# Two-level products for two of four blocks in groups 4 to 6 of a fused attention and feed-forward kernel on Trainium2

## The chip, the cores and the metric

The kernel runs on one NeuronCore of a Trainium2 chip. Its engines work from queues of their own: TensorE multiplies matrices (PE; its weight loads are listed as PEld), VectorE (DVE) and ScalarE (ACT) work on tensors and read the matmul results in PSUM, GpSimd (POOL) works on SBUF alone, and SyncE (SP) issues most transfers. The metric is the device time of the launch in microseconds (us), smaller being better.

## The reference, cut to what matters

```python
kv = np.einsum('bhsd,bhse->bhde', k, v)          # b, h, s, d = 8, 8, 576, 64
out = np.einsum('bhsd,bhde->bhse', q, kv)
rms = np.sqrt(np.mean(out * out, axis=-1, keepdims=True) + 1e-06)
x = (out / rms * g_norm)                         # -> (4608 tokens, 512)
a = x @ w1                                       # 512 -> 1024
b = x @ w2
return (a * b @ w3) @ w_out                      # 1024 -> 1024 -> 512
```

Everything is float32.

## The kernel before, in words

w3 @ w_out is multiplied out first (the first 83 us). Then come nine groups of 512 tokens: groups 0 to 7 hold 512 tokens of one batch each, and group 8 holds the 64 leftovers of all eight batches. Their order is 0 to 6, 8, 7.

**Gates.** A group first computes a and b (*gates*, line 770). The 1024 features are four *blocks* p = 0 to 3, each of two times 128 features. A block is a two-by-two product in Strassen-Winograd form: seven products instead of eight, over halves of features, of the contraction and of tokens. Per block that is 28 matmuls of 128x128 by 128x256 (line 646). ScalarE evicts banks into *late* tiles (*keep*, line 657), and VectorE adds, forms a * b (*multiply*, lines 784 and 785) and writes the pieces c12, c22, c11 and c21 of ab. The weights' sums s1, s2, s4 lie in tiles ws0 to ws3, and the tokens' sums t1 to t4 in xc (made by *combine_x*).

**Two blocks at two levels.** Groups 8 and 7 (TWICE) do block 2 in that form, then blocks 0 and 1 together in *gates_of_two* (line 851): the seven outer products are each split again into seven matmuls of 128x128 by 128x128, for w1 and then w2, 98 in all (line 875). The inner sums of tokens are made on GpSimd (*sum_x*, line 827). The inner sums of weights are made during groups 3 and 4 (*prepare_w*), stored in DRAM, and loaded back in parts of 896 KB (*load_w*); *replace_a21* makes the fourth kind in place in group 6. VectorE adds and combines the results (lines 893 to 910). Block 3 follows, with VectorE in written order.

**Projection.** The group then multiplies by w3 @ w_out at two levels (*project_twice*, line 1040, matmuls on line 1075), with weights streamed by *load_b*; VectorE makes sums of ab just ahead (*sum_inner*, lines 1033 to 1037).

**Attention of the next batch.** While group T runs, batch T + 1 is prepared in eight pieces (*steps*, line 519), which *between* (line 1302) puts between products, two in each block: k v products, the q kv product of each half (*finish*), and for odd batches that of two batches' leftovers (*product_left*). *norm* squares on ScalarE, reduces on VectorE, takes a root on ScalarE, a reciprocal and a product on VectorE. q and x are turned by DMA: a copy that parts 16-bit halves, a DMA transpose issued by SP, a copy back (*turn_by_dma*, lines 296 to 310); from batch 2 on all these copies are GpSimd's.

**Order.** TensorE, GpSimd and SP run in written order throughout. VectorE does in the last block and the projection of a group, and from gates_of_two on in groups 8 and 7. Elsewhere VectorE's and ScalarE's order is set when the kernel is built, by readiness and then by written order; *issue_after* keeps an instruction behind a named one of its engine. Tiles of a pool with one buffer make the next writer wait for the last reader; the pool *ps_mm* has five PSUM banks, and *ps_at* three.

## Time and profile before

| what | value |
|---|---|
| time, median of 3 runs | 758.19 us (758.11 to 759.98) |
| profiled execution: its own time, its span | 758.72 us, 756.9 us |
| group 4, gates (390.8 to 445.2), VectorE / ScalarE / GpSimd busy | 54.4 us, 38.85 / 16.09 / 22.79 us |
| group 5, gates (467.08 to 520.64) | 53.56 us, 30.32 / 15.15 / 19.75 us |
| group 6, gates (542.5 to 595.37) | 52.87 us, 33.83 / 15.06 / 20.90 us |
| group 5, projection (520.64 to 542.5) | 21.86 us, 20.63 / 5.12 / 0 us |
| DMA | 143.2 MB, mean 189 GB/s |

The profile is of one execution. A row of a group of instructions gives line, engine, operation, output and input by the program's names, shape and count; then busy time, mean time of one, and idle time ahead with its cause. The chain of waits goes back from the last instruction, at each step to what released it. Rows of busy time by stage give for each engine the busy time and, in brackets, the instructions; then the granted clock, the share of time the transfers took, and their GB/s. In the timeline the columns are start, duration, engine, line, operation, operands and shape.

### The profile page before, as it was taken

The page shows a single profiled execution, that of the slowest core. Times are in us where ns is not written, and L with a number is a line of the kernel's source. Part 1 is how long each engine was busy: PE and PEld are TensorE (multiplying, and loading weights), DVE is VectorE, ACT ScalarE, POOL GpSimd, SP SyncE. Part 2 cuts the span into 40 slices and gives each one's busy share as a digit, 9 for nine tenths or more (in the row PEclk, how much of TensorE's full clock was granted, in tenths as well). Part 3 has the DMA queues.
Part 4 walks back from the last instruction along what each step waited for, and adds up shares of the span by engine and source line. Part 5 has one row for each costly group of instructions (what it writes and reads, how often), then busy time and mean ns, then how long its engine had stood idle before and what let it go on. Part 6 is the DMA issues. An engine that isn't in the chain of part 4 may idle for free.

```text
span 756.9 us, 14948 instructions
## 1 busy us (share of the span) xinstructions
PE 749.4 (99%) x5903; PEld 657.7 (87%) x5903; DVE 589.4 (78%) x1171; ACT 267.0 (35%) x492; POOL 164.1 (22%) x190
## 2 busy tenths in 40 slices
PE   8999999999999999999999999999999999999998
PEld 5455788888899889988998899889988999999997
DVE  7977999639888568758975897567776778996897
ACT  6777787312322232223222322232223223222321
POOL 0000000322511441144114410431143124006000
PEclk9999999999999999999999999999999999999999
DMA  9996954349997845675767567745743470465244
GB/s 319 344 334 177 273 163 102 85 104 271 336 299 248 225 114 177 223 205 141 218 218 210 155 192 223 208 103 173 224 125 53 150 225 28 146 211 186 87 152 139
DMA packets 146554, 143.20 MB, mean 189 GB/s; under 512 B 86580, under 2 KB 133812, under 8 KB 146484
## 3 DMA queue, kind: packets, MB, share of 16 engines
q1 hardware_dynamic: 144032, 127.82, 58.1%
q10 hardware_dynamic: 2452, 14.42, 5.7%
q8 instruction: 47, 0.77, 0.4%
q14 instruction: 23, 0.19, 0.1%
HBM read 105.78 MB, written 19.14 MB: 165 GB/s over the span
## 4 chain that ended last, share of the span: by engine, by line
PE 97%; DVE 1%; DMA 1%; ACT 1%; issue 0%; SPq 0%; ACTq 0%
PE mm L646 55%; PE mm L1075 23%; PE mm L625 7%; PE mm L875 5%; PE at L339 3%; PE at L415 2%; PE at L612 1%; PE at L875 1%; DMA raw<-in_moe_w_out_dram 1%; PE at L1126 0%; DVE ab L163 0%; PE at L358 0%; PE at L434 0%; DVE chunks L170 0%; SPq L198 0%
## 5 line engine op out<-in xcount | busy, mean ns | idle before, releaser
L646 PE MATMUL mm<-xT,w_sb 128*128 128x256 f32 x720 | 165.2, 380 | 0.0
L646 PEld LDWEIGHTS mm<-xT,w_sb 128*128 128x128 f32 x720 | 136.6, 191 | 18.3 <-issue 0.5
L646 PE MATMUL mm<-xc,ws 128*128 128x256 f32 x512 | 116.2, 380 | 0.0
L646 PEld LDWEIGHTS mm<-xc,ws 128*128 128x128 f32 x512 | 97.3, 190 | 13.7 <-ACT p L659 0.8
L296 POOL COPY xT<-xn 128x1024 uint16<-128x1024 uint16 x26 | 31.2, 1227 | 171.9 <-DVE xn L393 171.9
L784 DVE TENSOR_TENSOR c<-mm,u 128x512 f32<-128x512 f32 x32 | 22.0, 689 | 58.4 <-PE mm L646 58.4
L659 ACT COPY u<-mm 128x512 f32<-128x512 f32 x58 | 34.0, 585 | 93.4 <-PE mm L646 82.8
L659 ACT COPY p<-mm 128x512 f32<-128x512 f32 x66 | 38.7, 586 | 73.9 <-PE mm L646 68.5
L646 PE MATMUL mm<-xc,w_sb 128*128 128x256 f32 x256 | 61.4, 383 | 0.0
L625 PE MATMUL mm<-chunks,ab 128*128 128x512 f32 x128 | 60.1, 603 | 1.0 <-DVE chunks L173 1.0
L646 PE MATMUL mm<-xT,ws 128*128 128x256 f32 x240 | 57.4, 383 | 0.0
L785 DVE TENSOR_TENSOR ab<-c 128x256 f32<-128x256 f32 x96 | 53.8, 561 | 2.5
L646 PEld LDWEIGHTS mm<-xc,w_sb 128*128 128x128 f32 x256 | 48.0, 190 | 6.9 <-ACT u L659 0.3
L646 PEld LDWEIGHTS mm<-xT,ws 128*128 128x128 f32 x240 | 45.1, 190 | 6.2
L1075 PE MATMUL mm<-w3o_sb,ab 128*128 128x128 f32 x368 | 48.7, 276 | 0.0
L1075 PE MATMUL mm<-w3o_sb,raw 128*128 128x128 f32 x372 | 48.1, 276 | 0.0
L384 DVE TENSOR_REDUCE inv<-sq 128x8 f32<-128x512 f32 (+1 forms) x40 | 23.4, 627 | 30.0 <-ACT sq L383 30.0
L1075 PEld LDWEIGHTS mm<-w3o_sb,ab 128*128 128x128 f32 x368 | 45.4, 192 | 0.5
L780 ACT COPY c<-mm 128x256 f32<-128x256 f32 x32 | 11.9, 372 | 95.4 <-PE mm L646 95.4
L1075 PEld LDWEIGHTS mm<-w3o_sb,raw 128*128 128x128 f32 x372 | 44.8, 192 | 0.0
L1086 ACT COPY u<-mm 128x512 f32<-128x512 f32 x23 | 13.5, 586 | 85.3 <-DVE raw L1099 46.6
L310 POOL COPY xT<-xn 128x1024 uint16<-128x1024 uint16 x26 | 31.6, 1244 | 54.0 <-DMA xn<-xT 54.0
(300 smaller groups left out, 1378.7 us busy)
## 6 DMA issues: line engine op xcount, KB each, us to landing
w3o_sb<-w3o_l SPq DMA_DIRECT2D x18, 896.0 KB, 5.4
raw<-in_moe_w_dram SPq DMA_DIRECT2D x31, 512.0 KB, 7.1
raw<-w3o_l SPq DMA_DIRECT2D x15, 896.0 KB, 4.7
w3o_sb<-w3o_l ACTq DMA_DIRECT2D x14, 896.0 KB, 4.6
k_sb<-in_k_dram SPq DMA_DIRECT2D x32, 256.0 KB, 4.5
v_sb<-in_v_dram SPq DMA_DIRECT2D x32, 256.0 KB, 4.7
q_sb<-in_q_dram SPq DMA_DIRECT2D x32, 256.0 KB, 3.3
out_dram<-raw SPq DMA_DIRECT2D x14, 512.0 KB, 4.3
```

Of the source, the lines that this page charges most:

```text
L296: copy(to, src.rearrange("p a n w -> p w a n"))
L310: copy(words(dst), src)
L339: nc.tensor.matmul(kv_ps[e * D:(e + 1) * D, r - rs[0], :], lhsT=k_sb[:, e, cols] if j < J else kl[:, 2 * r + e, :], rhs=v_sb[:, e, cols] i ...
L384: nc.vector.tensor_reduce(out=inv[:, i], in_=sq.rearrange("p (h d) -> p h d", d=D), axis=AX.X, op=ALU.add)
L415: nc.tensor.matmul(o_ps[l][tokens, n * D:(n + 1) * D], lhsT=qT[r][rows, e, i, tokens], rhs=kv_b[rows, e, r, :], start=True, stop=True,)
L625: nc.tensor.matmul(sums_ps[half][m], lhsT=w3T[half, c][:, m, :], rhs=chunks[:, c, 1, :], start=(c == 0), stop=(c == KF - 1),)
L646: nc.tensor.matmul(ps[:, u, :], lhsT=lhsT(a_name, u, c), rhs=rhs(b_name, c),  start=(u == 0 and c == 0 and to is None), stop=(c == chunks ...
L659: copies.setdefault(name, []).append(nc.scalar.copy(t, ps))
L784: adds.setdefault(name, []).append(nc.vector.tensor_add(c, one, two))
L785: nc.vector.tensor_mul(dst, c[:, 0, :], c[:, 1, :])
L875: nc.tensor.matmul(ps[place // 4][:, place % 4, :], lhsT=x, rhs=y, start=new and place // 4 not in seen, stop=True, skip_group_check=True,)
L1075: nc.tensor.matmul(to[:, i, :], lhsT=x[:, c, :], rhs=y[:, c, :], start=new and place // 4 not in seen, stop=(c == 1), skip_group_check=True,)
```

## The change

- Groups 4, 5 and 6 too take blocks 0 and 1 in *gates_of_two* (IN_TWO; block 2 first, then the two, then block 3). The eight pieces of attention lie there: two in block 2, after products 2 and 5 of each w in the two-level part, two in block 3.
- For batches 5 to 7 the copies of the turnings are ScalarE's, each behind a named bank copy (*turns_by_scalar*, *run_slot*). Leftovers' products of odd batches (5 and 7) move to the first piece of block 3. The copies of their turning stay GpSimd's.
- *sum_x* is eight VectorE operations in place of 28 of GpSimd, behind the last output add of the group before, into ws0, ws1 and a square buffer. For that, all inner weight blocks of outer s1, s2 and s4 are stored and loaded too: 66 blocks of 128 columns in five parts, three loaded ahead and two inside the stage.
- *gates_of_two* takes five banks of ps_mm, with none of ps_at, and only the late tiles p1, p5 and u.
- Squares have two named buffers up to batch 4 and one from batch 5 on.
- *prepare_w* runs in its seven steps, one at a time (two in one place), from group 1 to 3, and *replace_a21* in group 3.

The diff, cut to its core:

```diff
@@ -62,6 +62,7 @@
+    FIRST_OF_TWO = 4
...
@@ -359,27 +360,27 @@
-        def q_by_dma(r):
+        def q_by_dma(r, copy=None):
...
-            return turn_by_dma([q_sb], to, q_sb, [to], q_copy)
+            return turn_by_dma([q_sb], to, q_sb, [to], copy or q_copy)
...
-        def q_left_by_dma():
+        def q_left_by_dma(copy=None):
...
-            return turn_by_dma([src], to, src, [to], q_copy)
+            return turn_by_dma([src], to, src, [to], copy or q_copy)
         def norm(o_ps, dsts):
...
-                sq = work.tile([P, G], FP32, name="sq")[:, 0:w]
+                sq = work.tile([P, G], FP32, name=f"sq{0 if b > FIRST_OF_TWO else i}", bufs=1)[:, 0:w]
...
@@ -450,19 +451,18 @@
-        def x_by_dma(h, copy=nc.gpsimd.tensor_copy):
+        def x_part_by_dma(h, r, copy):
...
-            half = [slice(r * G, (r + 1) * G) for r in range(2)]
-            return together(
-                turn_by_dma(
-                    [xn[:, :, r * P:(r + 1) * P]], flat[:, half[r]], turned[:, half[r]], [x[:, :, r]],
-                    copy,
-                )
-                for r in range(2)
+            half = slice(r * G, (r + 1) * G)
+            return turn_by_dma(
+                [xn[:, :, r * P:(r + 1) * P]], flat[:, half], turned[:, half], [x[:, :, r]], copy
...
+        def x_by_dma(h, copy=nc.gpsimd.tensor_copy):
+            return together(x_part_by_dma(h, r, copy) for r in range(2))
...
@@ -516,6 +516,54 @@
         return batches[b]
+    slots, stage = {}, [None]
+    def run_slot(key, behind):
+        for f, *args in slots.pop(key, []):
+            with tc.issue_after(behind.ins):
+                f(*args)
+    def turns_by_scalar(b):
+        a, turning = batch(b), {}
+        def at(key, *call):
+            slots.setdefault(key, []).append(call)
+        def begin(name, f, *args):
+            turning[name] = f(*args, nc.scalar.copy)
+            next(turning[name])
+            if name[0] == "q":
+                next(turning[name])
+            elif name[2]:
+                for r in range(2):
+                    next(turning["x", name[1], r])
+        def end(name):
+            all_of(turning[name])
+            if name[0] == "q" and name[1] != "left":
+                batch(name[1]).load_ahead("q", name[2])
+        for r in (2, 3):
+            at((0, 0), begin, ("q", b, r), a.q_by_dma, r)
+        if b % 2:
+            at(("p2", "c21"), begin, ("q", "left"), a.q_left_by_dma)
+            at((0, 3), end, ("q", "left"))
+        at((0, 6), end, ("q", b, 2))
+        at((1, 0), end, ("q", b, 3))
+        for h, begins, ends in (
+            (0, ((0, 3), (0, 3)), ((1, 3), (1, 3))),
+            (1, (("p3", "p1"), ("p3", "p5")), (("p3", "c21"), ("proj", "p1"))),
+        ):
+            for r in range(2):
+                at(begins[r], begin, ("x", h, r), a.x_part_by_dma, h, r)
+                at(ends[r], end, ("x", h, r))
+        if b + 1 < B:
+            n = batch(b + 1)
+            for r in range(2):
+                at(("p3", "u2"), begin, ("q", b + 1, r), n.q_by_dma, r)
+                at(("proj", ("u2", "u3")[r]), end, ("q", b + 1, r))
...
@@ -543,6 +591,7 @@
         odd = b % 2
+        by_scalar = b > FIRST_OF_TWO
...
@@ -577,6 +626,8 @@
+        elif by_scalar:
+            turns_by_scalar(b)
         else:
...
@@ -587,16 +638,20 @@
         if odd:
-            fs[second].append((a.product_left,))
+            fs[6 if by_scalar else second].append((a.product_left,))
...
-            turn(5, a.x_by_dma, 1)
+            if not by_scalar:
+                turn(5, a.x_by_dma, 1)
             if odd:
-                turn(5, a.x_left_by_dma, next_group=more)
+                turn(7 if by_scalar else 5, a.x_left_by_dma, next_group=more or by_scalar)
+                if by_scalar and not more:
+                    slots["proj", "p5"] = [to_end.pop()]
+        if more and not by_scalar:
+            turn(7 if b == 1 else 5, batch(b + 1).q_two_by_dma, 0, 1, next_group=True)
         if more:
-            turn(7 if b == 1 else 5, batch(b + 1).q_two_by_dma, 0, 1, next_group=True)
             fs[7 if odd else 0].append((load_q_left, b + 1))
...
@@ -657,6 +712,7 @@
         def keep(name, ps):
...
+            run_slot((stage[0], name), copies[name][-1])
...
@@ -777,7 +833,8 @@
             if two is None:
...
-                nc.scalar.copy(c, one[:, 0, :])
+                copied = nc.scalar.copy(c, one[:, 0, :])
+                run_slot((stage[0], name), copied)
...
@@ -793,6 +850,24 @@
+    PRODUCTS = [
+        ("a11", "b11"), ("a12", "b21"), ("s2", "t2"), ("s1", "t1"), ("s3", "t3"), ("s4", "b22"),
+        ("a22", "t4"),
+    ]
+    BLOCKS = {}
+    for w in range(2):
+        for n, (name, _) in enumerate(PRODUCTS):
+            keys = ("a11", "a12", "a22", "s3") if name in ("s1", "s2", "s4") else ()
+            for key in (*keys, "s1", "s2", "s4"):
+                BLOCKS[w, n, key] = len(BLOCKS)
+    IN_PART = PART // P
+    W_PARTS = -(-len(BLOCKS) // IN_PART)
+    def store_w(n, key, src):
+        dst = w_l2[:, 0:len(BLOCKS) * P].rearrange("p (w m) -> p w m", w=2)
+        at = BLOCKS[0, n, key] * P
+        nc.sync.dma_start(out=dst[:, :, at:at + P], in_=src)
...
@@ -802,71 +877,76 @@
-            for i, s in enumerate((s1, s2, s4)):
-                at = (3 * n + i) * 2 * P
-                nc.sync.dma_start(
-                    out=w_l2[:, at:at + 2 * P].rearrange("p (w m) -> p w m", w=2), in_=s
-                )
+            blocks = {"s1": s1, "s2": s2, "s4": s4, "a11": a11, "a12": a12, "a22": a22}
+            for key, t in blocks.items():
+                if (0, n, key) in BLOCKS:
+                    store_w(n, key, t)
...
     def replace_a21():
-        for name, _ in PRODUCTS:
+        for n, (name, _) in enumerate(PRODUCTS):
...
+            if (0, n, "s3") in BLOCKS:
+                store_w(n, "s3", a21)
...
     def load_w():
...
+        if n == W_PARTS:
+            return
...
-        nc.sync.dma_start(out=t, in_=w_l2[:, n * PART:(n + 1) * PART])
+        t = t[:, 0:min(PART, len(BLOCKS) * P - n * PART)]
+        nc.sync.dma_start(out=t, in_=w_l2[:, n * PART:n * PART + t.shape[1]])
...
     def sum_x(T):
...
-            for name in ("k_sb", "v_sb", "q_sb"):
-                for _ in range(2):
-                    x_sums.append(inp.tile([P, 2, J * D], FP32, name=name))
-            x_sums.append(work.tile([P, 2, 2, P], FP32, name="qT"))
-            x_sums[:] = [
-                t.rearrange("p a b -> p (a b)") if len(t.shape) == 3 else
-                t.rearrange("p a b c -> p (a b c)") for t in x_sums
-            ]
-            x_sums[:] = [[t[:, i * P:(i + 1) * P] for i in range(4)] for t in x_sums]
-        nc.gpsimd.tensor_copy(tick, late["p1"][:, 0, 0:1])
-        for t, (_, name) in zip(x_sums, PRODUCTS):
-            b11, b12, b21, b22 = (
-                xb[T][name][:, c, i * P:(i + 1) * P] for c in range(2) for i in range(2)
-            )
-            t1, t2, t3, t4 = t
-            nc.gpsimd.tensor_sub(t1, b12, b11)
-            nc.gpsimd.tensor_sub(t2, b22, t1)
-            nc.gpsimd.tensor_sub(t3, b22, b12)
-            nc.gpsimd.tensor_sub(t4, b21, t2)
-    places = []
-    def gates_of_two(T):
-        if not places:
-            other = work.tile([P, 2, 2, NP // 2, N], FP32, name="xT")
-            other = other.rearrange("p i j r n -> p (i j r n)")
-            places.extend([other[:, 0:PART // 2], other[:, 1024:1024 + PART // 2]])
-            places[:] = [t.rearrange("p (n t) -> p n t", t=P) for t in places]
+            of_xc, of_xT = (free["w", p] for p in range(2))
+            of_xc, of_xT = (t.rearrange("p s w c m -> p (s w c m)") for t in (of_xc, of_xT))
+            x_sums.append([
+                *(of_xT[:, i * 4 * P:(i + 1) * 4 * P].rearrange("p (n t) -> p n t", t=P) for i in range(3)),
+                work.tile([P, G], FP32, name="sq1", bufs=1).rearrange("p (n t) -> p n t", t=P),
+            ])
+            x_sums.append([
+                of_xc[:, i * 3 * P:(i + 1) * 3 * P].rearrange("p (n t) -> p n t", t=P) for i in range(4)
+            ])
+        whole = xT[T].rearrange("p i j c n -> p (i j) c n"), xc
+        for (t1, t2, t4, t3), x in zip(x_sums, whole):
+            b11, b12, b21, b22 = (x[:, :, c, i * P:(i + 1) * P] for c in range(2) for i in range(2))
+            nc.vector.tensor_sub(t1, b12, b11)
+            nc.vector.tensor_sub(t2, b22, t1)
+            nc.vector.tensor_sub(t3, b22, b12)
+            nc.vector.tensor_sub(t4, b21, t2)
+    X_OUTER = {"b11": (0, 0), "t3": (0, 1), "b21": (0, 2), "b22": (0, 3), "t1": (1, 0), "t2": (1, 1), "t4": (1, 2)}
+    def gates_of_two(T, between=lambda: None):
+        mm = [bank(ps_mm, "mm").rearrange("p (i n) -> p i n", n=P) for _ in range(5)]
+        plan = [((0, 1), (2, 3), (4, 2)), ((3, 4), (2, 0), (1, 2))]
+        names = [("p1", "p5", "u2", "p1"), ("u2", "p5", "p1", "u2")]
...
-            a11, a12, s3, a22 = (t[:, w] for t in w_blocks(a_name))
-            s1, s2, s4 = (
-                loaded_w[q // 7][:, q % 7 * 2 * P + w * P:q % 7 * 2 * P + (w + 1) * P]
-                for q in range(3 * n, 3 * n + 3)
-            )
+            def block(key):
+                at = BLOCKS[w, n, key]
+                return loaded_w[at // IN_PART][:, at % IN_PART * P:(at % IN_PART + 1) * P]
+            if (w, n, "s3") in BLOCKS:
+                a11, a12, s3, a22 = (block(key) for key in ("a11", "a12", "s3", "a22"))
+            else:
+                a11, a12, s3, a22 = (t[:, w] for t in w_blocks(a_name))
+            s1, s2, s4 = (block(key) for key in ("s1", "s2", "s4"))
...
-            t1, t2, t3, t4 = x_sums[n]
+            of, i = X_OUTER[b_name]
+            t1, t2, t4, t3 = (t[:, i] for t in x_sums[of])
...
@@ -877,16 +957,23 @@
-            if w == 1 and n in (2, 4, 6):
-                load_b()
+            load(w, n)
+            if n in (2, 5):
+                between()
             return ps
-        def banks(pool, tag):
-            return [bank(pool, tag).rearrange("p (i n) -> p i n", n=P) for _ in range(2)]
-        def keep(t, ps):
+        def load(w, n):
+            last = max(at for (v, m, _), at in BLOCKS.items() if (v, m) <= (w, n))
+            if last + 1 >= (len(loaded_w) - len(streams) + 1) * IN_PART:
+                load_w()
+            if (w, n) == (1, len(PRODUCTS) - 1):
+                for _ in range(3):
+                    load_b()
+        def keep(name, ps, at):
+            t = late_tile(name)
...
-            nc.scalar.copy(t[:, 4:7], ps[1][:, 0:3])
+            run_slot(at, nc.scalar.copy(t[:, 4:7], ps[1][:, 0:3]))
...
@@ -910,15 +997,17 @@
         for w in range(2):
-            r1 = products(0, w, banks(ps_mm, "mm"), True)
-            p1 = keep(late_tile("p1"), r1)
-            r3 = products(1, w, banks(ps_at, "at"), True)
+            r1, r3, r2 = ([mm[i] for i in pair] for pair in plan[w])
+            of_p1, of_u2, of_p5, of_last = names[w]
+            products(0, w, r1, True)
+            p1 = keep(of_p1, r1, (w, 0))
+            products(1, w, r3, True)
...
-            z = keep(late_tile("u2"), r1)
-            r2 = products(3, w, banks(ps_mm, "mm"), True)
-            p5 = keep(places[1] if w else late_tile("p5"), r2)
+            z = keep(of_u2, r1, (w, 2))
+            products(3, w, r2, True)
+            p5 = keep(of_p5, r2, (w, 3))
...
@@ -926,7 +1015,7 @@
-            finish(keep(places[0], r1), w, 1, 0)
+            finish(keep(of_last, r1, (w, 6)), w, 1, 0)
...
@@ -1084,7 +1173,7 @@
         def keep(name, ps):
...
-            nc.scalar.copy(t[:, 4:7], ps[1][:, 0:3])
+            run_slot(("proj", name), nc.scalar.copy(t[:, 4:7], ps[1][:, 0:3]))
...
@@ -1096,7 +1185,7 @@
-            nc.vector.tensor_add(dst[:, 0], z[:, 3:6:2], z[:, 0:3:2])
+            adds["out"] = nc.vector.tensor_add(dst[:, 0], z[:, 3:6:2], z[:, 0:3:2])
...
@@ -1308,23 +1394,28 @@
-            if T == B - 2 and p == 2 and not replaced:
+            if T == FIRST_OF_TWO - 1 and p == 2 and not replaced:
...
-        if T in TWICE:
-            once = iter([T])
-            gates(T, 2, lambda: [sum_x(t) for t in islice(once, 1)])
-            run(sum_ab(2))
-            in_order = tc.manual_schedule(engines={mybir.EngineType.DVE})
-            in_order.__enter__()
-            gates_of_two(T)
+        if T in IN_TWO:
+            p = 2
+            stage[0] = "p2"
+            with tc.issue_after(adds["out"].ins):
+                sum_x(T)
+            gates(T, p, between)
+            run(sum_ab(p))
+            if T in TWICE:
+                in_order = tc.manual_schedule(engines={mybir.EngineType.DVE})
+                in_order.__enter__()
+            gates_of_two(T, between)
...
-            if T in TWICE and p + 1 < NF:
+            if T in IN_TWO and p + 1 < NF:
...
+            stage[0] = f"p{p}" if T in IN_TWO else None
...
@@ -1336,10 +1427,10 @@
-                if T in TWICE:
+                if T in IN_TWO:
...
-                else:
+                if T not in TWICE:
...
@@ -1381,13 +1472,13 @@
             else:
...
-                    for _ in range({(3, 1): 2, (3, 2): 2, (4, 1): 2, (4, 2): 1}.get((T, p), 0)):
+                    for _ in range({(1, 2): 1, (2, 0): 1, (2, 1): 1, (2, 2): 1, (3, 0): 1, (3, 1): 2}.get((T, p), 0)):
...
-                load_w if not last and groups[n + 1] in TWICE else load_b,
+                load_w if not last and groups[n + 1] in IN_TWO else load_b,
...
```

## The prediction

> **What bounds the kernel now.** I read the page's engine shares and slices first, then the chain of waits in order of time, then busy time by stage, then VectorE's own timeline around one stage that exists today in the form the change spreads. The page:
>
> ```profile
> PE 749.4 (99%) x5903; PEld 657.7 (87%) x5903; DVE 589.4 (78%) x1171; ACT 267.0 (35%) x492; POOL 164.1 (22%) x190
> ...
> PE 97%; DVE 1%; DMA 1%; ACT 1%; issue 0%; SPq 0%; ACTq 0%
> PE mm L646 55%; PE mm L1075 23%; PE mm L625 7%; PE mm L875 5%; PE at L339 3%; PE at L415 2%; PE at L612 1%; PE at L875 1%; DMA raw<-in_moe_w_out_dram 1%; PE at L1126 0%; DVE ab L163 0%; PE at L358 0%; PE at L434 0%; DVE chunks L170 0%; SPq L198 0%
> ```
>
> TensorE is the chain: 97% of it, and line 646, the one-level products, is 55%. From 80 us to 753 us I find no TensorE gap over 0.1 us. So matmul time taken away is gained in full unless a wait appears, and any wait is lost in full. The chain in order of time prices both forms, in the leftovers' group:
>
> ```profile
> 617.26 12.09 PE mm L646 x56
> 629.35 1.56 PE mm L875 x14
> 630.91 1.56 PE at L875 x14
> 632.47 9.38 PE mm L875 x84
> 641.85 1.56 PE at L875 x14
> 643.41 7.82 PE mm L875 x70
> 651.23 12.09 PE mm L646 x56
> 663.32 21.89 PE mm L1075 x196
> ```
>
> One block at one level takes 12.09 us (28 matmuls and 28 weight loads); two blocks at two levels take 651.23 - 629.35 = 21.88 us, 1.563 us for each of 14 products. By stage (columns: PE, weight loads, DVE, ACT, POOL busy):
>
> ```profile
> 629.35:651.23 21.88, 21.88 (x197) 21.88 (x197) 18.76 (x42) 8.40 (x16) 4.40 (x9) 1.00 0.24 81
> 651.23:663.32 12.09, 12.09 (x58) 10.67 (x58) 11.36 (x24) 2.23 (x4) 0.00 (x0) 1.00 0.31 92
> 663.32:685.20 21.88, 21.88 (x197) 21.88 (x197) 20.85 (x50) 5.11 (x10) 0.00 (x0) 1.00 0.68 235
> ```
>
> VectorE is busy for 50.97 of these 55.85 us, and this group has no attention beside it. Groups 4, 5 and 6 have. VectorE's timeline shows how little is left:
>
> ```profile
> 647.54 0.69 DVE L893 TENSOR_TENSOR xT<-mm,xT 128x512 f32<-128x512 f32 x1 [0.66 <-PE mm L875]
> ...
> 657.27 0.69 DVE L937 TENSOR_TENSOR raw<-raw,ab 128x512 f32<-128x512 f32 x1
> 658.25 0.69 DVE L784 TENSOR_TENSOR c<-mm,u 128x512 f32<-128x512 f32 x1 [0.28 <-PE mm L646]
> 658.97 0.43 DVE L785 TENSOR_TENSOR ab<-c 128x256 f32<-128x256 f32 x1
> 659.32 0.68 DVE L938 TENSOR_TENSOR ab<-ab 128x512 f32<-128x512 f32 x1
> 659.92 0.68 DVE L784 TENSOR_TENSOR c<-p,mm 128x512 f32<-128x512 f32 x1
> ```
>
> From 647.54 it has one idle moment over 0.1 us, of 0.28. The add at 659.92 (c22 of the last block) frees the bank of the last block's last product at 660.60; that product starts at 663.32 - 1.73 = 661.59. The cover in this stage is 0.28 + 0.99 = 1.27 us.
>
> **What the Trainium skill says.** "TensorE: Matmul & The Clock Gate", section on the array's architectural detail: VectorE and ScalarE queues are strictly first in, first out, so an instruction that waits holds all behind it. The trace agrees: in the 0.28 us before 658.25 VectorE idles for a bank, while the sum of line 938, whose inputs were done by 657.96, stands behind it until 659.32. "Perfetto Trace Analysis", Identifying the Most-Contended Engine: weight-load share says more than matmul share. Here that is 100% in the two-level stage against 10.67 of 12.09 us at one level, so I take 21.88 us as a floor that cannot be pressed. "SBUF — State Buffer", two separate sides: a VectorE operation with two SBUF inputs and a GpSimd operation exclude each other. The trace agrees: the same product of line 785 takes 0.43 us at 658.97, and 1.14 us at 432.11 with a GpSimd copy running. "DMA: Bandwidth & Descriptors", Issuing engines are not separate DMA queues: all transfers share 16 engines, so turnings queue beside the large loads; their median is 2.8 us today, and no run shows them beside the new loads.
>
> **The change part by part.** *Matmuls:* groups 4, 5 and 6 do blocks 0 and 1 at two levels: 3 x (2 x 12.09 - 21.88) = 3 x 2.30 = 6.9 us less. All other matmuls stay.
>
> *sum_x* goes from 28 GpSimd operations (9.3 us, in two groups) to 8 VectorE ones in five: four of 512 columns at about 0.65 and four of 384 at about 0.52 us, 4.7 us. They stand behind the previous group's last output add, where VectorE idles 4.42 us until 624.27. Cost nothing; without that cover, 0.3 us on an add with 1 us of slack.
>
> *Weights' sums and stores:* the same 21 operations, one to two groups earlier, and replace_a21 (7 operations, 4.8 us in group 6 today with no TensorE gap) now in group 3, where VectorE was busy 37.97 of 53.54 us. The stores grow from 21 to 33 blocks of 128 KB at 1.9 us, on SP. Hidden by that slack; uncovered, up to 0.5 us in group 3.
>
> *Loads of sums:* five parts rather than three, in five groups rather than two. Parts 4 and 5 are issued inside the stage: part 4 after its fourth product (6.3 us in), needed from the tenth (14.1 us); a part takes 5.0 us. Margin 2.8 us, and part 5 has more. The three load_b move from the sixth to the last product's end; the first is needed 12.1 us later and takes 5. Nothing.
>
> *Turning copies* of batches 5 to 7 go from GpSimd to ScalarE: 16 a batch at 1.05 us (apart) or 1.16 us (back), 17.7 us, plus 2.2 us for leftovers' q; ScalarE was busy 15.1 + 5.1 of 75 us. Each stands behind a named bank copy; the next such copy follows 1.5 to 4.7 us later in the two-level stage. The tightest is one back copy between the last eviction of the first w and the first of the second (1.07 + 1.16 us, where 1.56 and 1.5 of slack are to be had). Behind a waiting turning copy the queue holds evictions, for which TensorE waits; the transfer has 6 us or more against 2.8. I take nothing; 0 to 1 us a group.
>
> *Banks and late tiles:* all five mm banks and three late tiles now rotate. Checked against the leftovers' timeline: the tightest is the last product's tile, read until 655.91 and wanted by the last block's third copy at 656.45, 0.5 us. It yields when VectorE is late, together with the bank below.
>
> *Attention beside it, on VectorE:* this is the price. The norm of the second half comes after product 3 of the second w. Its TensorE work (1.31 + 1.09 us) gives VectorE room, but its chain is square 0.60, reduction 0.68, second square, which with one buffer waits for that reduction, second reduction, root 0.31, reciprocal 0.25, two products 1.25: about 4.6 us. The add of product 5 comes 2.5 us after the attention's matmuls. So the reciprocal and products, 1.45 us, and up to the second reduction, 0.7, fall into the saturated stretch: 1.45 to 2.15 us late, less 1.27 of cover, plus up to 0.3 for the first project product waiting on c11. Group 5: 0.2 to 1.2 us, I take 0.7.
>
> Groups 4 and 6 (odd batches) also have the leftovers' norm, now in the last block, where VectorE's order is the written one: two reductions 0.41, reciprocal 0.19, two products 0.41, overlapped 1.7 us, ahead of c12. Their matmuls give TensorE 0.8 us. Net 0.9, plus VectorE waiting inside it for the second square and root: 0 (if ScalarE's parts are early) to 1.4 us (0.38 + 0.30, four hand-overs of 0.1, and a running turning copy); GpSimd's copy of the leftovers behind it can stretch c12 by 0.5. Each 0.2 + 0.9 = 1.1 to 1.2 + 0.9 + 1.9 = 4.0; I take 2.3, a little under the middle, since the two waits are partly the same time.
>
> Sum: -6.9 + 0.7 + 2 x 2.3 = -1.6 us. The profiled execution took 758.72 us (span 756.9 and 1.8 around it), giving 757.1; the median of the runs is 0.5 lower, so **756.6 us**.
>
> **Rivals.** *VectorE finds room* (0.20): ScalarE's order runs the squares early and the late norm costs under 2.4 us in all. For it: VectorE is idle for 3.1 us of the leftovers' two-level stage. Against: none of it lies after 647.54. Time 758.19 - 6.9 + 0 to 2.4 = 751.3 to 753.7.
>
> *Leftovers' squares behind turning copies* (0.20), the slower end: the two copies of the next q stand just behind the third copy of the last block on ScalarE, 2 x 1.05 us, and the leftovers' squares behind them. The first square then ends about 9.6 us after the block's start, c12 starts at about 12.8 instead of 7.8, and each odd group loses 12.8 - 8.4 = 4.4 us (8.4 being where c12 costs nothing: 7.8 plus 0.99 of cover, less 0.4 for the first project product). With 0.7 that is 9.5: 760.8 us. It decides from 4.25 us an odd group. For it: the written order. Against: that third copy itself waits for VectorE, so a square may go ahead.
>
> *Turnings land late* (0.05): ScalarE's end copies wait for data queued behind the loads, evictions behind them, TensorE behind those; 2 us in three groups and the above, 762. Against: 6 us of distance for 2.8.
>
> **How the numbers follow.** My case has 0.55, its own range 753.7 to 760.5 (2.4 to 9.2 us of new waits: 0.2 + 2 x 1.1 to 1.2 + 2 x 4.0). About 0.3% (2.3 us) is what a measurement of this kernel can tell from no change: faster is below 755.9, slower above 760.5. Of my case 0.22 lies below 755.9 and 0.33 within. Faster 0.22 + 0.20 = 0.42; within 0.33 + 0.01 = 0.34; slower 0.20 + 0.04 = 0.24. The range 752.0 to 761.3 leaves out the lowest part of the second case and the highest of the others.
>
> **What would show it.** Right: three stages of 21.9 us plus 2.4 us of attention under the two-level line in groups 4 to 6; TensorE gaps only around the last block of these groups and the first project product, ended by VectorE (the c22 add) or by a bank copy that waited for a late tile; larger in groups 4 and 6 than in 5; VectorE without idle time from product 5 to the project. Wrong: no gaps (then near 751.3); gaps inside the two-level products ended by DMA or by evictions behind turning copies; gaps in groups 1 to 3 from the moved sums; or a product of the two-level stage over 1.6 us.

## The result, and the profile after

The changed kernel takes 766.40 us (median of 4 runs, 764.19 to 766.76) against 758.15 us before (758.0 to 759.98): a ratio of 1.0097, with a 95% interval of 1.0072 to 1.0122. It is 1% slower, where 756.6 us was forecast. Its profiled execution took 766.76 us with a span of 764.9 us, 8.0 us more than that of before, and the last matmul ends 8.04 us later (761.52 against 753.48).

The page after: the line of TensorE's busy share, and the lines of the chain that ended last.

```profile
PE 747.3 (98%) x6155; PEld 661.7 (87%) x6155; DVE 636.5 (83%) x1301; ACT 323.0 (42%) x558; POOL 82.5 (11%) x83
...
PE 85%; DVE 5%; DMA 4%; SPq 2%; POOL 1%; ACT 1%; issue 1%; ACTq 0%; DVEq 0%; POOLq 0%
```

TensorE is busy for 2.1 us less than before (747.3 against 749.4) in a span that is 8 us longer, and its share of the chain falls from 97% to 85%: other work now ends last somewhere. The two forms cost what they did. The chain in order of time, in the leftovers' group (start, duration, what):

```profile
625.30 12.09 PE mm L701 x56
637.39 21.89 PE mm L955 x196
...
671.36 21.88 PE mm L1164 x196
```

And busy time by stage there (PE, weight loads, DVE, ACT, POOL busy, granted clock, share of the transfers, GB/s):

```profile
637.40:659.30 21.90, 21.90 (x197) 21.90 (x197) 17.57 (x41) 8.42 (x16) 0.00 (x0) 1.00 0.33 107
659.30:671.20 11.90, 11.90 (x57) 10.47 (x56) 11.20 (x23) 2.24 (x4) 0.00 (x0) 1.00 0.49 177
671.20:693.10 21.90, 21.90 (x198) 21.90 (x197) 20.51 (x50) 5.12 (x10) 0.00 (x0) 1.00 0.68 235
```

Against the rows of before, GpSimd's part of the two-level stage is gone (4.40 to 0.00 us) and VectorE has 1.2 us less in it. So the saving in matmuls is there; the loss lies in other groups. Here are the lengths of the groups, from the end of one projection to the end of the next, by the starts of the matmuls in the two traces (us):

| group | before | after | difference | projection before, after |
|---|---|---|---|---|
| start and group 1 | 238.72 | 246.48 | +7.76 | 22.01, 29.43 |
| 2 | 76.50 | 76.80 | +0.30 | 21.88, 21.88 |
| 3 | 75.44 | 75.44 | 0 | 21.88, 21.88 |
| 4 | 76.26 | 78.25 | +1.99 | 21.88, 22.61 |
| 5 | 75.44 | 73.15 | -2.29 | 21.88, 21.88 |
| 6 | 74.73 | 75.01 | +0.28 | 21.89, 22.81 |
| 8 and 7 | 132.77 | 132.77 | 0 | |

Group 5 gains the whole 2.29 us of a two-level stage. Groups 4 and 6 should have done so too; they lose 4.28 and 2.57 us against that. The largest loss, 7.4 us, is in the projection of group 1, where no product was changed at all. (Of the other 0.34 us of the first row, 0.33 lie ahead of the first group's products, which begin at 83.37 against 83.04.)

**Group 1.** The chain of waits after, from the turning copies to the projection's first products:

```profile
208.68 4.32 SPq L301
...
213.04 5.38 SPq L301
...
219.87 1.25 SPq L301
...
221.22 2.11 DMA w_l<-raw
...
223.42 0.43 DVE raw L1122
...
223.89 9.87 PE mm L1164 x72
```

SyncE's queue stands in the chain: its transposes of x and q, then the store of the weights' sums out of tile raw, then a VectorE sum that writes a tile raw, then the products that need the sum. SyncE's timeline after, at the same place:

```profile
207.17 11.25 SPq L301 DMA_TRANSPOSE xn<-xT  x2
218.52 2.60 SPq L301 DMA_TRANSPOSE q_sb<-qT  x2
221.22 1.58 SPq L870 DMA_DIRECT2D w_l<-raw  x3
```

and VectorE's (a bracket gives the idle time ahead and what ended it):

```profile
210.65 0.42 DVE L879 TENSOR_TENSOR raw<-w_sb,raw 128x256 f32<-128x256 f32 x1
...
216.26 0.42 DVE L842 TENSOR_TENSOR ab<-c 128x256 f32<-128x256 f32 x1
223.42 0.42 DVE L1122 TENSOR_TENSOR raw<-ab 128x256 f32<-128x256 f32 x1 [6.73 <-DMA w_l<-raw]
```

The sums of the first of *prepare_w*'s seven steps are done at 211.07. Their three stores are issued 10 us later, since they stand on SyncE behind four transposes, two of which hold its queue for 11.25 us. The buffer they read is the one that the projection's first sum of ab writes, and that sum waits 6.73 us for it. TensorE stands still for 5.33 us. The transposes are not new. SyncE's timeline before:

```profile
208.11 10.26 SPq L300 DMA_TRANSPOSE xn<-xT  x2
218.47 2.61 SPq L300 DMA_TRANSPOSE q_sb<-qT  x2
```

Before, they held the queue for as long, with nothing behind them that anyone needed soon. What makes these transposes so slow was not followed: of the 11.25 us the profile puts 1.5 to a wait for GpSimd's copies, and the DMA engines were full at the time (transfer shares of 1.05 and 1.38 from 205 to 217 us). VectorE's timeline before shows when the projection's first sum was due:

```profile
216.37 0.43 DVE L1033 TENSOR_TENSOR raw<-ab 128x256 f32<-128x256 f32 x1
```

**Groups 4 and 6.** In group 4 the last block begins at 438.07, by the chain. ScalarE's timeline after:

```profile
443.33 0.59 ACT L714 COPY u<-mm 128x512 f32<-128x512 f32 x1 [0.24 <-PE mm L701]
443.82 1.99 ACT L299 COPY qT<-q_sb 128x1024 uint16<-128x1024 uint16 x2
445.71 0.39 ACT L384 ACTIVATE sq<-at 128x256 f32<-128x256 f32 x1
446.64 0.38 ACT L384 ACTIVATE sq<-mm 128x256 f32<-128x256 f32 x1 [0.55 <-DVE inv L385]
447.51 0.30 ACT L389 ACTIVATE inv<-inv,eps_col 128x8 f32<-128x8 f32 x1 [0.49 <-DVE inv L385]
```

and VectorE's, in written order:

```profile
444.23 0.68 DVE L1026 TENSOR_TENSOR raw<-raw,ab 128x512 f32<-128x512 f32 x1
446.13 0.42 DVE L385 TENSOR_REDUCE inv<-sq 128x4 f32<-128x256 f32 x1 [1.22 <-ACT sq L384]
447.06 0.42 DVE L385 TENSOR_REDUCE inv<-sq 128x4 f32<-128x256 f32 x1 [0.51 <-ACT sq L384]
447.85 0.20 DVE L391 RECIPROCAL inv<-inv 128x8 f32<-128x8 f32 x1 [0.37 <-ACT inv L389]
...
448.82 0.68 DVE L841 TENSOR_TENSOR c<-mm,u 128x512 f32<-128x512 f32 x1
449.54 0.80 DVE L842 TENSOR_TENSOR ab<-c 128x256 f32<-128x256 f32 x1
...
450.87 0.68 DVE L841 TENSOR_TENSOR c<-p,mm 128x512 f32<-128x512 f32 x1
```

The two turning copies of the next q stand ahead of the leftovers' first square; the second square waits for the reduction of the first, having only one buffer; VectorE idles 1.22, 0.51 and 0.37 us in the norm, and c12 (line 841, 448.82) starts 10.75 us after the block. The c22 add (450.87) frees the bank of the block's last product at 451.55, and TensorE had been waiting for it since 449.25. In group 6 there is no next q; c12 starts 9.47 us after the block (which begins at 588.15) and TensorE waits 1.15 us; another 0.92 us are lost in its projection.

```profile
597.62 0.68 DVE L841 TENSOR_TENSOR c<-mm,u 128x512 f32<-128x512 f32 x1
```

**A second price on the long gaps.** Busy time by stage around both gaps:

```profile
223.90:226.00 2.10, 2.10 (x10) 2.10 (x11) 2.05 (x6) 0.59 (x1) 0.00 (x0) 0.50 0.00 0
```

```profile
449.25:451.60 2.35, 0.01 (x2) 0.00 (x1) 2.28 (x5) 0.00 (x0) 0.82 (x1) 1.00 0.62 138
...
452.50:455.90 3.40, 3.40 (x14) 2.96 (x13) 3.26 (x8) 1.29 (x2) 0.00 (x0) 0.50 0.93 258
```

The granted clock fell to 0.50 just after each of them, by its records for 3.41 us (from 223.77 and from 452.46). Before, it was 1.00 all through, but for the last microsecond. The 1.15 us gap of group 6 was not followed by this.

### The profile page after: what moved, and what is told of

The parts are those of the page before. It is cut to its first block, busy times and chain, and to the rows that moved or that the text cites. A ratio compares the mean times of both kernels' runs of the same rounds, so it can differ in the third digit from the quotient of the medians.

```text
span 764.9 us, 15613 instructions
## 1 busy us (share of the span) xinstructions
PE 747.3 (98%) x6155; PEld 661.7 (87%) x6155; DVE 636.5 (83%) x1301; ACT 323.0 (42%) x558; POOL 82.5 (11%) x83
## 4 chain that ended last, share of the span: by engine, by line
PE 85%; DVE 5%; DMA 4%; SPq 2%; POOL 1%; ACT 1%; issue 1%; ACTq 0%; DVEq 0%; POOLq 0%
PE mm L701 37%; PE mm L1164 22%; PE mm L955 14%; PE mm L680 7%; PE at L340 2%; PE at L416 2%; SPq L301 2%; DMA raw<-in_moe_w_out_dram 1%; PE at L667 1%; DMA raw<-w3o_l 1%; DMA xn<-xT 1%; DMA q_sb<-qT 1%; DVE c L841 1%; POOL xT L297 0%; DVE inv L385 0%
## 5 line engine op out<-in xcount | busy, mean ns | idle before, releaser
L701 PE MATMUL mm<-xT,w_sb 128*128 128x256 f32 x576 | 132.2, 379 | 0.0
L701 PEld LDWEIGHTS mm<-xT,w_sb 128*128 128x128 f32 x576 | 108.8, 190 | 14.7 <-issue 0.5
L701 PE MATMUL mm<-xc,ws 128*128 128x256 f32 x416 | 94.5, 380 | 0.2 <-ACT p L714 0.2
L701 PEld LDWEIGHTS mm<-xc,ws 128*128 128x128 f32 x416 | 79.0, 190 | 11.5 <-ACT p L714 0.9
L701 PE MATMUL mm<-xc,w_sb 128*128 128x256 f32 x208 | 51.2, 390 | 3.5 <-DVE c L841 3.5
L701 PE MATMUL mm<-xT,ws 128*128 128x256 f32 x192 | 46.0, 382 | 0.0
L842 DVE TENSOR_TENSOR ab<-c 128x256 f32<-128x256 f32 x78 | 42.4, 544 | 2.1
L680 PEld LDWEIGHTS mm<-chunks,ab 128*128 128x128 f32 x128 | 21.8, 190 | 24.2 <-issue 16.4
L701 PEld LDWEIGHTS mm<-xT,ws 128*128 128x128 f32 x192 | 36.0, 190 | 5.0
L955 PE MATMUL mm<-ws,w3o_sb 128*128 128x128 f32 x250 | 38.5, 275 | 0.0
```

The source lines that it names most:

```text
L680: nc.tensor.matmul(sums_ps[half][m], lhsT=w3T[half, c][:, m, :], rhs=chunks[:, c, 1, :], start=(c == 0), stop=(c == KF - 1),)
L701: nc.tensor.matmul(ps[:, u, :], lhsT=lhsT(a_name, u, c), rhs=rhs(b_name, c),  start=(u == 0 and c == 0 and to is None), stop=(c == chunks ...
L842: nc.vector.tensor_mul(dst, c[:, 0, :], c[:, 1, :])
L955: nc.tensor.matmul(ps[place // 4][:, place % 4, :], lhsT=x, rhs=y, start=new and place // 4 not in seen, stop=True, skip_group_check=True,)
```

## The experiments

The theory after the result: (A) in group 1, the stores behind SyncE's transposes hold a buffer that the projection's first sum needs; (B) in groups 4 and 6, the leftovers' norm in written order makes c12 late, in three parts: turning copies ahead of the squares, one buffer for two squares, and the chain of the norm itself. The rivals are given with each run. The median of before was 758.81 us beside e1 to e4, 758.84 beside e5 to e7, 758.68 beside e8 and e9, and 758.70 beside e10.

**e1, another buffer.**

```diff
-            s1, s2, s4 = inner_sums[n % 3]
+            s1, s2, s4 = inner_sums[(n + 2) % 3]
```

> The changed kernel, but prepare_w takes its three sum buffers in an order shifted by two, so that the step made in group 1 writes the buffer that the projection needs third and not the one it needs first. The sums, the stores and their places in every queue stay. Theory (the projection's first sum waits until the late store has read its buffer): the 5.33 us gap of TensorE at the start of group 1's projection and the half clock after it go, 7.4 us, so about 759.0 us. Rival (the stores or the load on SyncE's queue themselves hold the projection back): the gap stays above 4 us and the time stays near 766.4.

Measured: 763.46 us (762.45 to 764.67), ratio 1.0057 (1.0039 to 1.0075). The chain of waits:

```profile
220.40 5.78 DMA w_l<-inner_sums
...
226.21 0.43 DVE inner_sums L1122
```

The wait moved with the buffer, from the first sum to the one that writes this tile: TensorE now stands 2.36 us at 224.33, and 0.58 us at 238.20. So the buffer is the thing waited for, and the stores are too late even for the sum that comes last of the three.

**e2, the first step made in group 2.**

```diff
-  {(1, 2): 1, (2, 0): 1, (2, 1): 1, (2, 2): 1, (3, 0): 1, (3, 1): 2}
+  {(2, 0): 2, (2, 1): 1, (2, 2): 1, (3, 0): 1, (3, 1): 2}
```

> The changed kernel, but the first step of prepare_w is made in group 2 beside the second and not in group 1. Theory (that step in that group is the whole loss there): the same as for the other buffer, about 759.0 us, with no TensorE gap over 0.2 us in group 1. Rival (the moved sums cost in any early group): the gap turns up in group 2, and the time stays above 763.

Measured: 760.26 us (758.48 to 761.72), 1.0015 (1.0008 to 1.0022). The large gap is gone; 0.90 us in group 1's projection (at 233.38, behind a load of weights that took 6.92 us to land) and a new one of 1.19 us in group 2 (at 258.94) are left. There two steps in one place put six sums on VectorE ahead of a reduction, three of them 1.25 us long beside GpSimd's copies and the others 0.41, and ScalarE, waiting for that reduction to take its root, held an eviction. The gaps of groups 4 and 6 stand as they were (2.33 and 1.15 us).

**e3, the next q's copies later.**

```diff
-                at(("p3", "u2"), begin, ("q", b + 1, r), n.q_by_dma, r)
+                at(("p3", "c21"), begin, ("q", b + 1, r), n.q_by_dma, r)
```

> The changed kernel, but ScalarE's two first copies of the next q's turning stand behind the last copy of block 3 (c21) and not behind its third. Theory (the leftovers' squares wait behind them in group 4, and VectorE, in written order, with them): group 4's gap falls from 2.34 to about 1.2 us, as in group 6, where no such copies stand ahead; the half clock after it goes too, 1.7 us; about 2.8 us together, 763.6 us. Group 6 stays at 1.15. Rival (VectorE's lateness alone sets the gap): group 4 keeps a gap over 2 us, and the time stays near 766.4.

Measured: 775.52 us (774.37 to 777.18), 1.0217 (1.0197 to 1.0237). The gap of group 4 fell from 2.34 to 1.01 us, as theory B had it, but the projections behind have new ones of 4.60 us (at 460.81) and 2.60 us (at 540.94). SyncE's timeline and the chain of waits show why:

```profile
453.32 2.61 SPq L301 DMA_TRANSPOSE q_sb<-qT  x2
456.03 0.84 SPq L1106 DMA_DIRECT2D xT<-w3o_l  x1
```

```profile
456.03 9.28 DMA xT<-w3o_l
...
465.44 4.58 PE mm L1164 x20
```

The transposes waited on SyncE for the later copies (4.9 us for ScalarE's), and the projection's load of weights, written behind them, waited with them; it then took 9.28 us to land, against a median of 5.0 in the changed kernel. Group 5's gap has the same shape: transposes at 534.01, the load at 536.68, landed after 6.75 us. It is the fault of group 1 once more: work in SyncE's written order behind a transpose that is late.

**e4, the moved step alone, in the kernel before.**

```diff
-  {(3, 1): 2, (3, 2): 2, (4, 1): 2, (4, 2): 1}
+  {(1, 2): 1, (3, 1): 2, (3, 2): 2, (4, 1): 1, (4, 2): 1}
```

> The kernel before, with one of the two steps of prepare_w of group 4's block 1 made in group 1's block 2 instead, as the changed kernel has it; nothing else. Theory: this one moved step of three sums and three stores is enough to give the gap in group 1's projection: 5 us of gap and 1.7 us of half clock, about 765 us. Rival (the changed kernel's other edits are needed for it): 758.2.

Measured: 765.35 us (764.3 to 766.69), 1.0083 (1.0061 to 1.0105). Three sums and three stores, moved by themselves, cost 6.5 us: a gap of 4.78 us at 218.46 and half the clock for 3.41 us from 223.37. The chain of waits is that of the changed kernel:

```profile
208.87 4.20 SPq L300
...
213.12 4.73 SPq L300
...
220.65 2.02 DMA w_l<-raw
...
222.76 0.44 DVE raw L1033
```

**e5, the steps spread over groups 2 and 3.**

```diff
-  {(1, 2): 1, (2, 0): 1, (2, 1): 1, (2, 2): 1, (3, 0): 1, (3, 1): 2}
+  {(2, 0): 1, (2, 1): 2, (2, 2): 1, (3, 0): 1, (3, 1): 2}
```

> The changed kernel, with no step of prepare_w in group 1: one in group 2's block 0, two in its block 1, the others where they are. It is the base of the two runs sent with it. Theory (the 1.19 us gap of the earlier run, with two steps in block 0, came from six sums that ran against GpSimd's copies and held up a norm): no gap over 0.3 us in groups 1 to 3, 2.33 and 1.15 us left in groups 4 and 6, time 758.5 to 759.5 us. Rival (any double step in group 2 holds up the norm): a gap of about 1 us moves to block 1 or 2.

Measured: 758.48 us (757.73 to 760.91), 0.9997 (0.9988 to 1.0006). No gap over 0.1 us is left in groups 1 to 3, and 7.9 us are won back against the changed kernel. Groups 4, 5 and 6 take 78.24, 73.15 and 74.99 us, as after.

**e6, e5 with the next q's copies behind the leftovers' squares in group 4.**

```diff
-                nc.scalar.activation(sq, o_ps[i], AF.Square)
+                copies["sq"] = nc.scalar.activation(sq, o_ps[i], AF.Square)
...
+            if b > FIRST_OF_TWO:
+                run_slot(("p3", "left"), copies["sq"])
...
-                at(("p3", "u2"), begin, ("q", b + 1, r), n.q_by_dma, r)
+                at(("p3", "left" if b % 2 else "u2"), begin, ("q", b + 1, r), n.q_by_dma, r)
```

> The run e5, and the next q's two copies on ScalarE are put behind the leftovers' squares in group 4 instead of ahead of them; they stay in block 3, early. Theory (squares behind copies, VectorE in written order behind the squares): group 4's gap falls from 2.33 to 1.0 to 1.4 us, as in group 6, which stays at 1.15; no new gap in the projection, since the turnings' transfers still leave SyncE before the projection's loads; about 1.1 us below e5 (2.8 if the half clock came there). Rival (VectorE's work alone): no difference in group 4.

Measured: 757.38 us (756.72 to 758.72), 0.9978 (0.997 to 0.9986). Group 4 goes from 78.24 to 76.16 us, its gap from 2.34 to 1.36 us, and the clock stays at 1.00. Group 6 is unmoved (75.00 us): it has no next q.

**e7, e6 with two halves of the buffer for the leftovers' two squares.**

```diff
+                if b > FIRST_OF_TWO and n * w <= G:
+                    both = both if i else work.tile([P, G], FP32, name="sq0", bufs=1)
+                    sq = both[:, i * w:(i + 1) * w]
+                else:
...
-                sq = work.tile([P, G], FP32, name=f"sq{0 if b > FIRST_OF_TWO else i}", bufs=1)[:, 0:w]
+                    sq = work.tile([P, G], FP32, name=f"sq{0 if b > FIRST_OF_TWO else i}", bufs=1)[:, 0:w]
```

> The run e6, and the leftovers' two squares of 256 columns take the two halves of the one square buffer, so that the second does not wait for the first one's reduction. Theory (0.51 us of VectorE's wait in the chain is that buffer): the gaps in groups 4 and 6 fall by 0.5 us each, to about 0.6, and the time by 1 to 1.3 us below e6, to about 756.5. Rival (root and hand-overs take up what is freed): less than 0.4 us below e6.

Measured: 755.75 us (755.26 to 756.32), 0.996 (0.9946 to 0.9975): 0.4% faster than before. Group 4 takes 75.22 us and group 6 74.39; the gaps are 0.42 and 0.54 us. VectorE's timeline in group 4:

```profile
437.03 0.74 DVE L389 TENSOR_REDUCE inv<-sq 128x4 f32<-128x256 f32 x2
438.13 0.20 DVE L395 RECIPROCAL inv<-inv 128x8 f32<-128x8 f32 x1 [0.37 <-ACT inv L393]
...
439.12 0.68 DVE L847 TENSOR_TENSOR c<-mm,u 128x512 f32<-128x512 f32 x1
```

Of the three idle moments only the one for the root is left, 0.37 us; reductions, reciprocal and products still stand ahead of c12.

**e8, e7 without the leftovers' norm.**

```diff
-            all_of(norm(o_ps, [xn[:, :, e:e + 1, :] for e in range(2)]))
+            if b > FIRST_OF_TWO:
+                for e in range(2):
+                    src = o_ps[e].rearrange("p (m k d) -> p m k d", k=1, d=D)
+                    copies["sq"] = nc.scalar.copy(xn[:, :, e:e + 1, :], src)
+            else:
+                all_of(norm(o_ps, [xn[:, :, e:e + 1, :] for e in range(2)]))
```

> The kernel of e7 in which the leftovers of batches 5 and 7 get no norm: ScalarE copies their two products, and squares, sums, root, reciprocal and the two products with it are left out, so the outputs of these leftovers are not those of the reference. My theory: this chain, written ahead of c12 on VectorE, is all that still holds groups 4 and 6. Then their gaps ahead of the project's first product (0.42 and 0.54 us in e7) are gone, group 4 takes 74.0 to 74.3 us and group 6 72.5 to 72.8, and the time is 752.5 to 753.5 us. The rival: VectorE is full in the last block for other reasons (the copies and sums of the two-level stage); then gaps over 0.4 us stay and the time stays above 754.5.

Measured: 752.35 us (752.18 and 752.51; just under the expected 752.5), 0.9916 (0.9896 to 0.9936). No TensorE gap over 0.1 us is left from 80 us on; group 4 takes 73.97 us, exactly its 76.26 of before less 2.29, and group 6 73.01. VectorE now waits for TensorE ahead of c12:

```profile
437.50 0.69 DVE L852 TENSOR_TENSOR c<-mm,u 128x512 f32<-128x512 f32 x1 [1.00 <-PE mm L712]
```

So in group 4 of e7 nothing but this norm stood against the gain. In group 6 0.57 us of the loss remain (expected 72.5 to 72.8), 0.36 of them in its projection; their cause wasn't followed.

**e9, e7 with the leftovers' reciprocal and products behind the projection's first sum.**

```diff
-            all_of(norm(o_ps, [xn[:, :, e:e + 1, :] for e in range(2)]))
+            steps_left = norm(o_ps, [xn[:, :, e:e + 1, :] for e in range(2)])
             if b > FIRST_OF_TWO:
+                next(steps_left)
+                next(steps_left)
+                rest_of_left.append(steps_left)
...
+                    slots["proj", "p1"].append((begin_left,))
...
                         lambda: sum_inner(0, lambda: all_of(f() for f in (sum_2, sum_3))),
+                        lambda: all_of(rest_of_left.pop() if rest_of_left else []),
```

> The kernel of e7 with the leftovers' norm cut in two: squares, reductions and root stay in the last block, while the reciprocal and the two products come behind the project's first sum; the turning of the leftovers then begins behind the project's first product. My theory: VectorE's c12 comes 0.6 us sooner, so group 4 goes from 75.2 to about 74.3 us, group 6 from 74.4 to about 73.2, and the time to 753.8 us. The rival: the later turning makes the projection wait for the leftovers' transposes or for loads that stand behind them; then the gap moves into group 6's projection and the time is 755 us or more.

Measured: 755.03 us (753.84 to 756.41), 0.9957 (0.994 to 0.9974): by the time, the rival's case. VectorE's timeline in group 4:

```profile
436.51 0.74 DVE L391 TENSOR_REDUCE inv<-sq 128x4 f32<-128x256 f32 x2
437.54 0.69 DVE L867 TENSOR_TENSOR c<-mm,u 128x512 f32<-128x512 f32 x1 [0.28 <-PE mm L727]
```

c12 again waits for TensorE, and group 4 takes 74.21 us, as expected. Group 6 takes 73.74 where 73.2 was expected: a gap of 0.58 us now lies in its projection (at 607.96), and the chain of waits leads to it through 16 us of VectorE operations without a pause over 0.4 us, the moved ones ahead of them. Groups 5 and 8 are each 0.23 us longer than in e7. Either theory was right in one group. The four executions fall in two pairs, 753.84 and 753.88 us at a mean granted clock of 1.000, 756.17 and 756.41 at 0.998; only one of the first pair was profiled. The median is not shown to be better than that of e7, since the intervals overlap.

**e10, the changed kernel with the first step's stores issued by ScalarE.**

```diff
-        nc.sync.dma_start(out=dst[:, :, at:at + P], in_=src)
+        queue = nc.sync if n else nc.scalar
+        queue.dma_start(out=dst[:, :, at:at + P], in_=src)
```

> The changed kernel with one edit: the three stores of the first step of weights' sums are issued by ScalarE's queue, not by SyncE's; where the step stands, its buffer and everything in groups 4 to 6 stay as they are. My theory: the stores were late only because they stood behind the four transposes on SyncE. Then they go out at about 211 us, the buffer is free by 214, the project's first product of group 1 waits for nothing, its projection takes 21.9 to 22.4 us instead of 29.4, clock included, and the time is 758.5 to 759.7 us. The rival: the stores were late because the 16 DMA engines were full of loads at that moment, whichever queue issues them; then they still land after 220 us, the gap stays over 3 us and the time is 763 us or more.

Measured: 761.44 us (760.29 to 766.07), 1.0031 (1.0013 to 1.005); the profiled execution was the longest of the six, so its trace may show more waiting than most. The median is 5.0 us better than the changed kernel, and 1.7 us above the expected range. ScalarE's timeline and then the chain of waits:

```profile
211.35 0.41 ACTq L871 DMA_DIRECT2D w_l<-raw  x1
211.81 0.58 ACT L714 COPY p<-mm 128x512 f32<-128x512 f32 x1 [4.86 <-DVE raw L755]
```

```profile
211.35 8.50 DMA w_l<-raw
```

The stores went out at 211.35, as the theory had it, and the projection's first sum waited for none of them: 0.33 and 0.29 us remain of the 5.33. But the first store took 8.50 us to land instead of 2.11, at a transfer share of 1.00, so the rival's mechanism is real too. In this run the sum was due only at 222.53, since TensorE had lost time ahead of it; in the changed kernel it was due at 216.68, and a store landing 8.5 us after 211.35 would still have come 3.2 us late for it. TensorE's gap, from 218.56, would then have been about 1.9 us instead of 5.33 (an estimate from these rows: its first product began 0.57 us after the landing). So the place in the queue was the larger part, full transfers the smaller. And the edit made a wait of its own: the stores wait on ScalarE for VectorE's sums, with an eviction behind them (the 4.86 us of idle time above), and TensorE lost 2.45 us at 209.99 and then half the clock for 3.41 us.

## Why the prediction was wrong, and where it was right

**The step that failed** is the one of the weights' sums and stores: "Hidden by that slack; uncovered, up to 0.5 us in group 3." It measured 7.4 us, in group 1. The slack that was named is VectorE's in group 3, while the first step went to group 1. VectorE did have room there: the sums themselves cost nothing in group 1. (In group 2, TensorE has a gap of 0.20 us at 264.79 behind three of these sums, each of 1.14 to 1.19 us ahead of a reduction.) The stores were given a duration (1.9 us each, "on SP") and no place in SyncE's queue. The row that answers it was in the trace of before, two transposes that hold SyncE for 10.26 us from 208.11 and two more to 221.08, just where the first step was moved. The other half was in the code: the tiles *inner_sums* serve both the weights' sums and, from 216.37 on in that trace, the projection's sums, so a store that is late keeps VectorE, and by it TensorE, from starting. e1, e4, e5 and e10 show each link. The prediction also named "gaps in groups 1 to 3 from the moved sums" as what would prove it wrong; that is what came.

**Matmuls**, 6.9 us less, 2.30 a group: right. Group 5 shows 2.29 us, e8 shows it in group 4, and 1.72 of it in group 6.

**sum_x on VectorE, the loads in five parts, the other turning copies on ScalarE**, each at nothing: no TensorE gap over 0.1 us lies in a two-level stage of groups 4 to 6. These stages take 24.49, 24.49 and 23.17 us: 21.88, and 2.61, 2.61 and 1.29 for the attention's matmuls and the changes to them and back. (The 9.3 us given for GpSimd's sums are their part in block 2 alone; with 4.40 in the two-level stage it was 13.7 us a group. Nothing depended on it.)

**The norm of the second half**, 0.7 us in group 5: it cost nothing there. c12 came 7.0 us after the block began, well ahead of 8.4. In group 6 the chain of waits does run back through VectorE to this norm (its first reduction, at 584.00); what it cost there was not tested.

**The odd groups**, 2.3 us each: they lost 4.28 and 2.57. The point from which a late c12 costs time, 8.4 us after the block's start, was right: 10.75 - 8.4 = 2.35 against a gap of 2.34, 9.47 - 8.4 = 1.07 against 1.15, and in e7 (the block begins at 430.28, c12 at 439.12) 0.44 against 0.42. That agreement is in part luck. The 8.4 takes off 0.4 us for the first product of the projection, but the gaps stand ahead of the block's last product; what took about 0.4 us there is the product on line 842, 0.80 us long while GpSimd copies the leftovers (1.04 us from 449.03), and 0.42 in e8. The prediction had that copy as a separate term. The rival "leftovers' squares behind turning copies" described group 4: that copies went ahead is what happened, though c12 came at 10.75 and not at 12.8. Its reason against, that a square may go ahead of the copies, did not hold. The runs, one trace each, split group 4's 4.28 us into four: 1.1 for the clock (77.14 us in e2, with the same gap and no drop, against 78.24 in e5), 1.0 for the copies ahead of the squares (the rest of e5 to e6), 0.94 for the one buffer (e6 to e7), 1.25 for the norm itself (e7 to e8). In group 6 the buffer was worth 0.61 and the norm 1.38; 0.57 stay open.

**The sum.** The forecast was -6.9 + 0.7 + 4.6 = -1.6. Measured against the whole saving it is -6.9 + 7.8 (the start and group 1, 7.4 of them in its projection) + 0.3 (group 2) + 4.3 + 2.6 = +8.1, where the traces have 8.04. Without the 7.4 us it would have been about +0.6, within the range; e5, which has not got them, measured 758.48 us. So the likeliest case was 2.3 us too low in the two odd groups together (6.9 against 4.6), 0.7 too high in group 5, and blind in group 1. Even without group 1 the change would have gained nothing that can be told from before: 758.48 us against 758.84.

## What to carry to other kernels

When a step is moved, follow its stores through the queue that issues them as closely as its arithmetic through its engine: ask what stands ahead of them there, how long that holds the queue, and who writes next to the buffer that they read. A transpose on SyncE that is slow, as in group 1, or waits for a copy, as in e3, holds every load and store behind it, and giving these to an engine that evicts for TensorE trades one wait for another. What a norm costs in a full stage of VectorE is set not only by its own operations, but by what stands ahead of its squares on ScalarE and by how many buffers the squares have: in group 4 these two were worth 1.9 us and the norm itself 1.25, in group 6 the buffer 0.61 and the norm 1.38.

## What the runs showed of the hardware that was not expected

After long gaps TensorE's clock was granted at half. All four gaps of 3.81 to 5.33 us, and six of eight between 2.33 and 2.60 us, were followed by half the clock for 3.41 or 6.83 us, beginning 2.2 to 5.2 us after the gap's start; none of the ten gaps of 1.0 to 1.4 us were. The Trainium skill, in "TensorE: Matmul & The Clock Gate", Part 1 on the clock gate, has the half clock after at least one idle window of about 3.4 us, with a window that runs freely. The 3.41 us agree; six of the gaps that it followed were shorter than that window, down to 2.33 us, and of two gaps of the same length at the same place (e2 and e5) one was followed by it and the other not. It also seems to differ between executions of one kernel: of e2's 20, 8 have a mean granted clock of 1.000 and a median of 759.0 us, 12 have 0.998 and 760.4. What decides it was not found. In group 4 it cost about 1.1 us, in the last block and the start of the projection together.

The same skill, in "DMA: Bandwidth & Descriptors", under Issuing engines are not separate DMA queues, says that initiating transfers on several engines only saves the sequencer's time, "which is usually small relative to the DMA itself". Here it was not small: two transposes held SyncE for 11.25 us, and a store that takes 2.11 us went out 10 us late. That all share the same 16 engines agrees with e10, where the store took 8.50 us.
